# One attention order on one core: first unit turned by VectorE alone, scores by halves, fewer and longer weighing groups

## The chip, the cores and the metric

The kernel runs on one core of a Trainium2 chip. The metric is the device time of the whole program in microseconds (us), read over several runs. Within the core, TensorE (PE; its weight loads are listed apart as PEld) multiplies and transposes, VectorE (DVE), ScalarE (ACT) and GpSimd (POOL) do elementwise work, and SyncE (SP) issues every DMA, one after another, on one queue (SPq). Each engine works through its own list in order, so an instruction that waits holds up everything behind it on that engine.

## The reference, cut to what matters

Rotary attention over 4 batches and 8 heads of 576 positions and 64 dimensions, then two feed-forward stages on 2304 tokens:

```
q_rot, k_rot = rotate(q), rotate(k)                 # x1*cos - x2*sin, x1*sin + x2*cos
scores = q_rot @ k_rot^T / 8;  attn = softmax(scores)
x = (attn @ v) as 2304 x 512
h = x @ w_in; g = elu(h); x = g @ w_out             # 512 -> 2048 -> 512
out = ((x @ w1) * (x @ w2)) @ w3 @ w_out2           # 512 -> 1024 -> 512
```

All of it is float32. The kernel splits an operand into a rounded high part and a remainder (hi, lo) and multiplies hi*hi + hi*lo + lo*hi, which is why most products stand as three matmuls or as stacked operands.

## The kernel before, in words

The program has two stages. The attention stage (lines 140 to 509) has an order written out by hand; the feed-forward stage (from line 512) is placed by a planner and follows when the attention is nearly done. Only the attention stage is touched.

A **unit** is one batch and one pair of heads (j = 0, 1): there are 16, in the list `units`. A unit has nine **score groups** g = (unit, c, j): four blocks of 128 queries for each head, and one last group (c = 4) that takes the remaining 64 queries of both heads. The list `seq` has all 144 groups, and slot n of the loop at lines 496 to 509 belongs to `seq[n]`. In slot n the loop writes out, in this order: the copies of the last slot's transposes out of PSUM (`evacuate_all`, five of twelve on ScalarE, the rest on VectorE); the steps due first in slot n; in the first slots some warming matmuls on zeros (`FILL`, `warm_up`); the scores and softmax of group n + 2 (`AHEAD` = 2, and the score tiles `ps_s` have two buffers); the other steps due in slot n; the transposes of group n (`turn`, tile ptp, and ptl for the remaining 64 keys).

The softmax of a group is a maximum on VectorE (line 298, tile nm) and an exponential with its sum on ScalarE (line 302, tile pr). `norm` (lines 357 and 358) takes the reciprocal of the sums on VectorE, `spread` widens it on GpSimd (rb, line 84), `norm_turn` transposes that on TensorE (ptr), and `weigh` multiplies the turned probabilities with v into the tile o: line 392 for key blocks 0 to 3 (two heads beside each other, each 64 columns of the array), line 394 for the rest of both heads, line 397 for the 64 last queries. `weighed` scales o into xT on VectorE. `PV` says in which slot of a unit which key blocks are weighed, for the first half of the queries (256) and the second (320). Slots are counted from the unit's own first slot; slot 9 is slot 0 of the next unit.

The scores of units 1 to 15 read a stacked copy (`stack`, tile st) of the rotated q and k (hl): the hi and lo parts of one head are put above each other on 128 partitions by eight DMAs per unit from SBUF to SBUF (lines 260 and 263). Only unit 0, and the last group of each unit, read hl itself (line 278); unit 0 does so with 64 rows of the array.

The rotation is done by GpSimd for units 2 to 15 (`rope`, tile raw_qk: two multiplications, line 184, an addition, line 187; then ScalarE rounds to hi, line 80, and GpSimd subtracts for lo, line 193). `ROPE` gives the slots of these five steps for q and for k, relative to the unit before. Before, k's remainder is due in slot 2 and q's in slot 4, and the eight DMAs of the stack follow in slot 4 (`STACK`). Unit 0 is rotated by pieces (`first_rope`, `part`): k's columns 0 to 352 and q's 0 to 256 by VectorE, k's columns 420 to 640 and q's 256 to 576 by GpSimd, k's 352 to 420 by VectorE. Unit 1's k is rotated by GpSimd, its q by VectorE.

SP's queue also carries the loads of q and k two units ahead (`LOAD_QK`, line 167, ring of three buffers, so a load waits until an older tile has been read), v (line 171), and one block of feed-forward weights per unit (line 91), which ScalarE, VectorE and GpSimd convert in six steps (`paced`, `STEPS`).

At the very start TensorE runs 27 warming matmuls (two passes each) on a tile of zeros while the first loads and rotations run.

## Time and profile before

| | |
|---|---|
| device time, three runs | 1053.31 us median, 1046.85 to 1053.48 |
| profiled execution | 1052.59 us, span 1050.8 us |
| busy share: PE, PEld, DVE, ACT, POOL | 99%, 82%, 54%, 44%, 25% |
| chain that ended last | PE 90%, SPq 3%, DMA 3%, DVE 1%, POOL 1% |
| attention stage | from the start to 320 us of the span, its end among the first feed-forward work |

The span runs from the first to the last instruction of one profiled execution; 1.79 us of its own time lie around it. Shares are means over two unlike stages. In the attention stage four engines and the DMA queues work side by side, in the feed-forward stage TensorE works almost alone. "Idle before" names what an engine waited for; a wait is charged to what came last. Busy time of TensorE includes the filling and emptying of its pipeline, so the distance from one start to the next is the better measure of what a group of matmuls costs.

### The profile page before, as it was taken

How to read it: one execution, taken by the hardware profiler on the slowest of the kernel's cores; microseconds unless marked ns; L12 is line 12 of the kernel's file. 1: busy time of each engine (PE TensorE's matmuls, PEld its weight loads, DVE VectorE, ACT ScalarE, POOL GpSimd, SP SyncE). 2: the span in 40 equal slices, each digit the busy share in tenths (PEclk: the TensorE clock that was granted, in tenths of full speed). 3: DMA queues.
4: the chain of work that ended last, by engine and by line, in shares of the span. 5: the costliest groups of instructions: out<-in, count | busy, mean ns of one | idle time of the engine just before them, and what ended most of it. 6: DMA issues, size and time to landing. Idle time of an engine off the chain costs nothing.

```text
span 1050.8 us, 14641 instructions
## 1 busy us (share of the span) xinstructions
PE 1037.8 (99%) x5590; PEld 865.4 (82%) x5590; DVE 568.3 (54%) x978; ACT 463.7 (44%) x921; POOL 257.9 (25%) x260
## 2 busy tenths in 40 slices
PE   8999999999999999999999999999999999999998
PEld 7767767777777888888888999989888888889997
DVE  4678878778767996668667653212313214122321
ACT  2567666667546756556545644322211212112121
POOL 4698889888510010001000000000100000000000
PEclk7799999999999999999999999999999999999999
DMA  4687878786756015545555523536400101001000
GB/s 157 190 233 213 232 221 216 211 236 198 172 211 242 1 40 180 180 160 180 181 180 180 181 101 127 193 120 220 143 0 1 41 1 41 1 1 41 1 31 31
DMA packets 46390, 138.84 MB, mean 132 GB/s; under 512 B 5488, under 2 KB 7152, under 8 KB 46320
## 3 DMA queue, kind: packets, MB, share of 16 engines
q1 hardware_dynamic: 46320, 137.91, 41.6%
q8 instruction: 44, 0.72, 0.3%
q14 instruction: 26, 0.21, 0.1%
HBM read 85.66 MB, written 25.69 MB: 106 GB/s over the span
## 4 chain that ended last, share of the span: by engine, by line
PE 90%; SPq 3%; DMA 3%; DVE 1%; POOL 1%; issue 1%; ACTq 0%; ACT 0%; DVEq 0%
PE h L537 19%; PE y L564 19%; PE a L537 9%; PE b L537 9%; PE y L674 9%; PE ptp L334 6%; PE o L392 5%; PE s L286 5%; PE w L615 4%; DMA st<-hl 3%; PE s L278 2%; SPq L263 2%; SPq L260 1%; PE o L394 1%; POOL hl L193 1%
## 5 line engine op out<-in xcount | busy, mean ns | idle before, releaser
L537 PE MATMUL h<-xt,w 128*128 128x512 f32 (+1 forms) x960 | 213.4, 368 | 0.0
L564 PE MATMUL y<-g,w 128*128 128x512 f32 (+1 forms) x960 | 212.5, 367 | 0.0
L537 PEld LDWEIGHTS h<-xt,w 128*128 128x128 f32 x960 | 175.2, 188 | 23.4 <-DVE e L552 0.2
L564 PEld LDWEIGHTS y<-g,w 128*128 128x128 f32 x960 | 175.2, 188 | 22.5
L76 POOL TENSOR_TENSOR xt<-xT,xt 128x512 fp32r<-128x512 f32 (+1 forms) x20 | 26.5, 1326 | 668.9 <-DVE xt L82 668.1
L302 ACT ACTIVATE pr<-s,nm 128x576 f32<-128x576 f32 x144 | 107.0, 743 | 100.8 <-DVE nm L298 99.9
L661 DVE TENSOR_TENSOR a<-b,a 128x512 f32<-128x512 f32 (+1 forms) x40 | 25.5, 637 | 180.0 <-PE b L537 180.0
L298 DVE TENSOR_REDUCE nm<-s 128x1 f32<-128x576 f32 x144 | 108.6, 754 | 25.7 <-PE s L286 11.7
L537 PE MATMUL a<-xt,w 128*128 128x512 f32 (+1 forms) x480 | 107.4, 368 | 0.0
L537 PE MATMUL b<-xt,w 128*128 128x512 f32 (+1 forms) x480 | 106.8, 367 | 0.0
L674 PE MATMUL y<-W,g 128*128 128x512 f32 x432 | 104.9, 390 | 0.0
L334 PEld LDWEIGHTS ptp<-idt,pr 128*128 128x128 f32 x576 | 63.4, 144 | 46.2 <-issue 23.7
L286 PE MATMUL s<-st 128*128 128x288 f32 x480 | 94.9, 316 | 4.4 <-DMA st<-hl 4.3
L537 PEld LDWEIGHTS a<-xt,w 128*128 128x128 f32 x480 | 88.2, 188 | 12.5
L537 PEld LDWEIGHTS b<-xt,w 128*128 128x128 f32 x480 | 87.7, 188 | 11.3
L334 PE MATMUL ptp<-idt,pr 128*128 128x128 f32 x576 | 96.4, 291 | 0.0
L674 PEld LDWEIGHTS y<-W,g 128*128 128x128 f32 x432 | 80.9, 188 | 16.1
L659 ACT ACTIVATE a<-a 128x512 f32<-128x512 f32 (+1 forms) x40 | 22.3, 556 | 139.2 <-PE a L537 139.2
L552 DVE SCALAR_TENSOR_TENSOR e<-e,h 128x512 f32<-128x512 f32 (+1 forms) x80 | 50.3, 631 | 61.1 <-ACT e L550 60.7
L184 POOL TENSOR_TENSOR raw_qk<-raw_qk,tab 128x640 f32<-128x640 f32 (+1 forms) x56 | 82.5, 1483 | 2.3
L549 ACT ACTIVATE e<-h 128x512 f32<-128x512 f32 (+1 forms) x80 | 44.2, 554 | 72.6 <-PE h L537 70.2
L286 PEld LDWEIGHTS s<-st 128*128 128x128 f32 x480 | 67.9, 189 | 7.0 <-issue 3.8
(301 smaller groups left out, 1275.0 us busy)
## 6 DMA issues: line engine op xcount, KB each, us to landing
kept<-w SPq DMA_DIRECT2D x40, 512.0 KB, 2.6
w<-kept SPq DMA_DIRECT2D x40, 512.0 KB, 3.3
st<-hl SPq DMA_DIRECT2D x60, 288.0 KB, 4.5
raw<-w_ SPq DMA_DIRECT2D x32, 512.0 KB, 3.6
raw_qk<-k_ SPq DMA_DIRECT2D x15, 640.0 KB, 6.1
raw_qk<-q_ SPq DMA_DIRECT2D x15, 576.0 KB, 5.1
st<-hl SPq DMA_DIRECT2D x60, 144.0 KB, 4.2
raw<-w_in_ SPq DMA_DIRECT2D x16, 512.0 KB, 5.1
```

What stands on the lines that cost most here:

```text
L184: pool.tensor_tensor(r[:, z], r[:, z], tab[:, w, z, TAB[w]], op=ALU.mult)
L286: pe.matmul(s[:, n, :288], st[:, j, 0, c * P:c * P + P], st[:, j, z, n * 288:(n + 1) * 288], start=(z == 1), stop=(z == 2),)
L298: dve.tensor_reduce(nm, s[:, :, :288], axis=AX.XY, op=ALU.max, negate=True)
L302: act.activation(pr_t[u, c][:, j].rearrange("p (n i) -> p n i", n=2), s[:, :, :288], ACTF.Exp, bias=nm, accum_out=sums_t[u, hf][:, at_:at_ ...
L334: pe.transpose(pt[:, kc], pr[:, at_:at_ + P], idt)
L392: pe.matmul(o[64 * j:64 * j + 64], vj[:, j, kc], th[:, j, kc], start=(kc == 0), stop=False)
L537: pe.matmul(ps[:, :n], w[:, a, cc * P:(cc + 1) * P], x[cc][:, c], start=(i == 0), stop=(i == 11))
L549: act.activation(e, ps[:, :n], ACTF.Relu, scale=-1.0)
L552: dve.scalar_tensor_tensor(g, e, -1.0, ps[:, :n], op0=ALU.add, op1=ALU.max)
L564: pe.matmul(ys[ti][o][:, :n], wout[f][:, a, o * P:(o + 1) * P], g[:, c], start=(f == 0 and i == 0), stop=(f == NF - 1 and i == 2),)
L615: pe.matmul(ps, w3_t[i, j // 4][:, a, j % 4 * P:j % 4 * P + P], wo[j][:, c], start=(j == 0 and n == 0), stop=(j == 7 and n == 2),)
L674: pe.matmul(outs[ti][o], g[:, a, o * P:(o + 1) * P], wW[f][:, c], start=(f == 0 and i == 0), stop=(f == NG - 1 and i == 2),)
```

## The change

The order of the attention stage is rewritten in these places. Unit 0 is rotated by VectorE alone. `scores` runs the three products of one half of the keys before those of the other half, and in the very first group four warming matmuls stand between the halves; there are 30 instead of 27 warming matmuls at the start and 4, 2, 2, 2, 2 instead of 4, 2, 2 in the first slots. The stack is filled by twelve DMAs of 144 KB: eight for k right after k's remainder (now due two slots before the unit ahead begins), four for q right after q's remainder (slot 3). Each load of q or k follows the stack's DMAs that set its buffer free. The weighing goes from four groups per half to two, with the rest of the keys inside the second, in slots 6, 8, 10 and 12; the last 64 queries use 128 rows, half of them zeros. Tile o has one buffer, the transposes three. `norm` and the first `spread` come one slot later, and the weights' conversion is spread over slots 0 to 10 of its run.

```diff
@@ -25,26 +25,25 @@
 
 
 
-NORM = (2, 7)
-SPREAD = (3, 9)
+NORM = (3, 8)
+SPREAD = (4, 9)
 NTURN = (5, 11)
 PV = (
-    (5, 0, (0,)), (6, 0, (1,)), (7, 0, (2, 3)), (8, 0, (4,)),
-    (10, 1, (0,)), (11, 1, (1,)), (12, 1, (2, 3)), (13, 1, (4,)),
+    (6, 0, (0, 1)), (8, 0, (4, 2, 3)), (10, 1, (0, 1)), (12, 1, (4, 2, 3)),
 )
 LOAD_V = 6
-LOAD_QK = 4
-ROPE = ((-1, 0, 1, 1, 4), (-5, -4, -3, -3, 2))
-STACK = 4
+FIRST_LOADS = ((0, 2, 1), (3, 2, 0), (5, 3, 1))
+ROPE = ((-1, 0, 1, 1, 3), (-5, -4, -3, -3, -2))
+DIAG = 5
 
 FIRST = ((0, 1, 4), (0, 0, 0, 1, 2), (0, 0, 3, 3, 4), 2)
-KD = 420
-WARM = 27
-FILL = (4, 2, 2)
+WARM = 30
+FILL = (4, 2, 2, 2, 2)
+FILL_IN = 4
 EVAC_ACT = (1, 0, 0, 1, 0, 0, 0, 0, 1, 0, 1, 0)
 
 
-PF, PF_AT, PF_STEP, STEPS, DLEAD = 6, 10, 9, (0, 1, 2, 2, 3, 8), 6
+PF, PF_AT, PF_STEP, STEPS, DLEAD = 6, 10, 9, (0, 2, 5, 7, 8, 10), 6
 NA = 2 * PF
 
 EARLY, EARLY_STEP, STAGES = 17, 1, 3
@@ -150,12 +149,13 @@
         x_p = pool1("x", 2)
         sm_p = pool1("sm", 4)
         ps_s = c1.enter_context(tc.tile_pool(name="ps_s", bufs=2, space=PSUM, reuse_waits="tile"))
-        ps_o = c1.enter_context(tc.tile_pool(name="ps_o", bufs=2, space=PSUM, reuse_waits="tile"))
-        ps_t = c1.enter_context(tc.tile_pool(name="ps_t", bufs=2, space=PSUM, reuse_waits="tile"))
+        ps_o = c1.enter_context(tc.tile_pool(name="ps_o", bufs=1, space=PSUM, reuse_waits="tile"))
+        ps_t = c1.enter_context(tc.tile_pool(name="ps_t", bufs=3, space=PSUM, reuse_waits="tile"))
 
         tab = tab_p.tile([P, 2, 2, SK], F32, name="tab")
         diag = [cst.tile([P, 2, P], F32R, name=f"diag{i}") for i in range(2)]
         two = cst.tile([P, D], F32, name="two")
+        pl1 = cst.tile([P, 384], F32, name="plT1")
         zero = cst.tile([P, 1, 1], F32, name="zero")
         rb = [cst.tile([P, 2, 2, D], F32, name="rb"), cst.tile([P, 3, 2, D], F32, name="rb2")]
 
@@ -191,8 +191,11 @@
 
             def low():
                 pool.tensor_tensor(lo, r[:, 0], hi.bitcast(F32), op=ALU.subtract)
-                if w == 0:
-                    diagonal(u)
+                stack(u, w)
+
+                m = units.index(u) + 2 - w
+                if m < len(units):
+                    load(units[m], 1 - w)
 
             return [lambda: turn(0), lambda: turn(1), add, high, low]
 
@@ -235,9 +238,7 @@
         def first_rope(u):
             for w, at_, to, eng, steps in (
                 (1, 0, 352, dve, (0, 1, 2)), (0, 0, 256, dve, (0, 1, 2)),
-                (1, 0, 352, dve, (3, 4)), (0, 0, 256, dve, (3, 4)),
-                (1, KD, SK, pool, (0, 1, 2)), (1, 352, KD, dve, (0, 1, 2)), (1, 352, SK, dve, (3, 4)),
-                (0, 256, S, pool, (0, 1, 2)),
+                (1, 0, 352, dve, (3, 4)), (0, 0, 256, dve, (3, 4)), (1, 352, SK, dve, (0, 1, 2, 3, 4)),
             ):
                 pieces = part(u, w, at_, to, eng, act, eng)
                 for k_ in steps:
@@ -249,18 +250,17 @@
                 h = slice(64 * j, 64 * j + 64)
                 copy_hi(diag[units.index(u) % 2][h, :, h], hls[u][h, :, 512:S].bitcast(F32), pool)
 
-        def stack(u):
-
-            st = stacks[u] = st_p.tile([P, 2, 3, S], F32R, tag="st", name="st")
+        def stack(u, w):
+
+            if u not in stacks:
+                stacks[u] = st_p.tile([P, 2, 3, S], F32R, tag="st", name="st")
+            st = stacks[u]
             for j in range(2):
-                c = (SK, S)[j]
-                for e in range(2):
-                    part = hls[u][64 * j:64 * j + 64, e].bitcast(F32)
-                    both = part[:, :2 * c].rearrange("p (w c) -> p w c", w=2)[:, :, :S]
-                    nc.sync.dma_start(st[64 * e:64 * e + 64, j, 0:2].bitcast(F32), both)
-                for e in range(2):
-                    part = hls[u][64 * j:64 * j + 64, 1 - e].bitcast(F32)
-                    nc.sync.dma_start(st[64 * e:64 * e + 64, j, 2].bitcast(F32), part[:, c:c + S])
+                c = (0, (SK, S)[j])[w]
+                for z in ((0,), (1, 2))[w]:
+                    for e in range(2):
+                        part = hls[u][64 * j:64 * j + 64, (e, 1 - e)[z == 2]].bitcast(F32)
+                        nc.sync.dma_start(st[64 * e:64 * e + 64, j, z].bitcast(F32), part[:, c:c + S])
 
 
         HALF = ((0, 256), (256, 320))
@@ -273,8 +273,10 @@
 
                 d, h = diag[units.index(u) % 2], slice(64 * j, 64 * j + 64) if c < 4 else slice(0, P)
                 at_ = S + 64 * (c == 4 or j == 0)
-                for i, (a, e) in enumerate(PAIRS):
-                    for n in range(2):
+                for n in range(2):
+                    if n and g == seq[0]:
+                        warm_up(FILL_IN)
+                    for i, (a, e) in enumerate(PAIRS):
                         pe.matmul(
                             s[:, n, :288], hls[u][h, a, c * P:c * P + P] if c < 4 else d[:, a],
                             hls[u][h, e, at_ + n * 288:at_ + (n + 1) * 288], start=(i == 0), stop=(i == 2),
@@ -325,7 +327,7 @@
             if j == 0 and c in (0, 2):
                 pt_t[u, hf] = [
                     pt_p.tile([P, 2, 4, nq], F32, tag=f"pt{hf}", name="ptT"),
-                    pt_p.tile([P, nq + 64 * hf], F32, tag=f"pl{hf}", name="plT"),
+                    pl1 if hf else pt_p.tile([P, nq], F32, tag="pl0", name="plT"),
                 ]
             (th, tl), pr = pt_t[u, hf], pr_t[u, c].rearrange("p j i -> p (j i)")
             pt = ps_t.tile([P, 4, P], F32, tag="pt", name="ptp")
@@ -380,25 +382,28 @@
 
         o_t = {}
 
-        def weigh(n, u, hf, kc):
+        def weigh(n, u, hf, kcs):
             nq = HALF[hf][1]
-            if kc == 0:
+            if kcs[0] == 0:
                 o_t[u, hf] = ps_o.tile([P, nq], F32, tag="o", name="o", padded_shape=[P, 512])
             o = o_t[u, hf]
             th, tl = pt_t[u, hf]
             vj = vs[u][:, :2 * NKC * D].rearrange("p (j k d) -> p j k d", j=2, k=NKC)
-            if kc < 4:
+            for kc in kcs:
+                if kc == 4:
+                    pe.matmul(o[:, :256], vs[u][:, 2 * NKC * D:], tl[:, :256], start=False, stop=False)
+                    if hf:
+
+                        for j in range(2):
+                            pe.matmul(
+                                o[64 * j:64 * j + 64, 256:], vj[:, j, 4], tl[:, 256 + 64 * j:320 + 64 * j],
+                                start=False, stop=False,
+                            )
+                    continue
                 for j in range(2):
-                    pe.matmul(o[64 * j:64 * j + 64], vj[:, j, kc], th[:, j, kc], start=(kc == 0), stop=False)
-                return
-            pe.matmul(o[:, :256], vs[u][:, 2 * NKC * D:], tl[:, :256], start=False, stop=not hf)
-            if hf:
-                for j in range(2):
-                    pe.matmul(
-                        o[64 * j:64 * j + 64, 256:], vj[:64, j, 4], tl[:64, 256 + 64 * j:320 + 64 * j],
-                        start=False, stop=True,
-                    )
-            at(n + 1, weighed, u, hf)
+                    pe.matmul(o[64 * j:64 * j + 64], vj[:, j, kc], th[:, j, kc], start=(kc == 0), stop=(kc == 3))
+            if kcs[-1] == 3:
+                at(n + 1, weighed, u, hf, first=True)
 
         def weighed(u, hf):
             n0, nq = HALF[hf]
@@ -419,7 +424,7 @@
 
             at(max(0, n - DLEAD), fetch)
             for i, d in enumerate(STEPS):
-                at(n + d, step, i, first=i in (0, 4, 5))
+                at(n + d, step, i, first=i in (0, 4))
 
         units = [(b, hp) for b in range(B) for hp in range(4)]
         order = [(c, j) for c in range(4) for j in range(2)] + [(4, 0)]
@@ -431,36 +436,36 @@
 
         for i, u in enumerate(units):
             n = 9 * i
-            if i + 2 < len(units):
-                at(n + LOAD_QK, load, units[i + 2], 1)
-                at(n + LOAD_QK, load, units[i + 2], 0)
+            if i == 0:
+                for d, ahead, w in FIRST_LOADS:
+                    at(d, load, units[ahead], w)
             if i + 1 < len(units):
                 v_ = units[i + 1]
                 at(n + LOAD_V, load_v, v_)
                 if i == 0:
                     steps = part(u, 0, 256, S, dve, act, dve)
-                    for k_ in (3, 4):
-                        at(FIRST[0][k_ - 3], steps[k_])
+                    for k_ in range(5):
+                        at(FIRST[0][max(k_ - 3, 0)], steps[k_])
                     at(FIRST[0][2], diagonal, u)
                     for w in (1, 0):
                         steps = part(v_, w, 0, (S, SK)[w], (dve, pool)[w], act, (dve, pool)[w])
                         for k_, d in enumerate(FIRST[2 - w]):
                             at(d, steps[k_])
                     at(FIRST[2][4], diagonal, v_)
-                    at(FIRST[2][4], stack, v_)
+                    at(FIRST[1][4], stack, v_, 1)
+                    at(FIRST[2][4], stack, v_, 0)
                 else:
                     for w in (1, 0):
                         at(n + ROPE[w][0], lambda v_=v_, w=w: steps_of.__setitem__((v_, w), rope(v_, w)))
                         for k_, d in enumerate(ROPE[w]):
                             at(n + d, lambda v_=v_, w=w, k_=k_: steps_of[v_, w][k_]())
-                    at(n + STACK, stack, v_)
+                    at(n + DIAG, diagonal, v_)
             for hf in range(2):
                 at(n + NORM[hf], norm, u, hf)
                 at(n + SPREAD[hf], spread, u, hf)
                 at(n + NTURN[hf], norm_turn, u, hf)
             for t, hf, kcs in PV:
-                for kc in kcs:
-                    at(n + t, weigh, n + t, u, hf, kc)
+                at(n + t, weigh, n + t, u, hf, kcs)
         at(4, lambda: pool.tensor_tensor(two, idt[:, :D], idt[:, D:], op=ALU.add))
         at(FIRST[3], lambda: pool.tensor_scalar(tab[:, 0], tab[:, 1], SCALE, 1.0, op0=ALU.mult, op1=ALU.mult))
         for i in range(2 * PF):
@@ -489,6 +494,7 @@
                 copy_hi(d, zero.to_broadcast([P, 2, P]), pool)
             first_rope(units[0])
             pool.memset(rb[1][:, 2], 0.0)
+            pool.memset(pl1[64:, 256:], 0.0)
             for g in seq[:AHEAD]:
                 scores(g)
                 softmax(g)
```

## Rows read from the trace of the kernel before

**Rows 1.** Windows: length, busy us (instructions) per engine, PEclk, DMA share, GB/s.
```profile
10.00:20.00 10.00, 7.38 (x31) 6.46 (x32) 5.25 (x8) 2.36 (x6) 7.58 (x8) 0.60 0.27 91
20.00:30.00 10.00, 10.00 (x40) 8.33 (x38) 6.03 (x11) 3.92 (x10) 3.73 (x5) 0.50 0.39 123
30.00:40.00 10.00, 10.00 (x41) 7.06 (x40) 4.99 (x8) 3.62 (x10) 6.15 (x7) 0.54 0.66 148
...
150.00:200.00 50.00, 48.69 (x353) 35.41 (x351) 39.64 (x73) 34.00 (x79) 42.52 (x41) 1.00 0.78 214
...
11.00:12.00 1.00, 0.00 (x0) 0.00 (x0) 0.97 (x2) 0.00 (x0) 0.95 (x2) 0.97 0.00 0
```

**Rows 2.** Timeline of the first 45 us: start, length, engine, line, work.
```profile
1.05 8.22 PE L475 MATMUL warm<-warm 128*128 128x128 f32 x54 [1.05 <-DVE warm L486]
9.21 0.40 PE L278 MATMUL s<-hl 64*128 64x288 f32 x1
9.74 1.48 DVE L215 TENSOR_TENSOR raw_qk<-raw_qk,tab 128x68 f32<-128x68 f32 x2
12.62 2.46 PE L278 MATMUL s<-hl 64*128 64x288 f32 x11 [3.02 <-ACT hl L80]
...
19.53 1.42 DVE L215 TENSOR_TENSOR raw_qk<-raw_qk,tab 128x576 f32<-128x576 f32 x2
...
40.07 0.76 PE L286 MATMUL s<-st 128*128 128x288 f32 x4
```

**Rows 3.** Timeline of TensorE in the steady units.
```profile
63.05 0.76 PE L392 MATMUL o<-ptT,v__388 128*64 128x320 f32 x4
...
188.44 0.76 PE L392 MATMUL o<-ptT,v__2018 128*64 128x320 f32 x4
...
203.80 0.78 PE L286 MATMUL s<-st 128*128 128x288 f32 x4
204.41 0.66 PE L334 MATMUL ptp<-idt,pr 128*128 128x128 f32 x4
204.83 0.76 PE L286 MATMUL s<-st 128*128 128x288 f32 x4
205.52 0.76 PE L392 MATMUL o<-ptT,v__2251 128*64 128x320 f32 x4
206.21 0.66 PE L334 MATMUL ptp<-idt,pr 128*128 128x128 f32 x4
...
209.50 1.30 PE L392 MATMUL o<-ptT,v__2251 128*64 128x320 f32 x8
210.73 0.66 PE L334 MATMUL ptp<-idt,pr 128*128 128x128 f32 x4
...
211.97 0.59 PE L394 MATMUL o<-plT,v__2251 128*128 128x256 f32 x2
212.49 0.33 PE L397 MATMUL o<-plT,v__2251 64*64 64x64 f32 x4
...
292.67 0.76 PE L392 MATMUL o<-ptT,v__3405 128*64 128x320 f32 x4
```

**Rows 4.** Waits from 40 to 300 us: us in total, times, longest.
```profile
PE s L286 <- DMA st<-hl: 4.3, 10, 0.9
...
POOL rb L84 <- DVE ri L358: 35.2, 22, 8.0
```

**Rows 5.** DMA issues of the page: KB each, median us from issue to landing.
```profile
st<-hl SPq DMA_DIRECT2D x60, 144.0 KB, 4.2
```

**Rows 6.** Stack DMAs on SP's queue, 60 to 300 us: issue ns min/median/max.
```profile
L260 SPq DMA_DIRECT2D st<-hl x52: 596/638/984, 66.2 to 283.3; - x52
...
L263 SPq DMA_DIRECT2D st<-hl x52: 597/1242/1450, 68.7 to 285.3; - x52
```

**Rows 7.** Costliest groups of the page: busy us, mean ns, idle before.
```profile
L302 ACT ACTIVATE pr<-s,nm 128x576 f32<-128x576 f32 x144 | 107.0, 743 | 100.8 <-DVE nm L298 99.9
...
L298 DVE TENSOR_REDUCE nm<-s 128x1 f32<-128x576 f32 x144 | 108.6, 754 | 25.7 <-PE s L286 11.7
```

## The prediction

> **What bounds the kernel now.** I read the windows by stretch first, then the timeline of the start, then TensorE's timeline and the waits in the steady part. The windows show that the attention has two regimes. From about 11 us to nearly 40 us the granted clock is 0.50, the 1.2 GHz level, while TensorE is busy all the time from 12.62 us on; in the steady windows it is 1.00 [rows 1, 2]. The timeline shows how the clock was lost: the warming matmuls end at 9.27 us, one score matmul follows, and then TensorE waits 3.02 us for ScalarE's rounding of k's second part; the clock falls inside that gap. Unit 1's first scores come at 40.07 us, 27.45 us after the restart [rows 2].
>
> In the steady part TensorE sets the pace. The first group of a unit's second half comes at 63.05 us and 13 units later at 292.67 us, so a unit takes 17.66 us; one without a wait takes 17.08 us (188.44 to 205.52) [rows 3]. The difference, 0.58 us a unit or 7.6 us over the 13, is TensorE late for the stacked operands: the only wait listed for it is on st, 4.3 us in ten pieces, and the rest hides in the pipeline's ends [rows 4]. GpSimd is busy 42.52 of 50 us, VectorE 39.64, ScalarE 34.00, the DMA engines 0.78 [rows 1]: per unit of 17.66 us that is 15.0, 14.0, 12.0 and 13.8 us. Nothing else is at its limit, but GpSimd and VectorE are near enough to matter if TensorE gets faster. After the attention TensorE is always fed, so what the attention saves should arrive whole at the end.
>
> The sum below is made against the profiled execution, 1052.59 us, which is 0.72 us under the median of the runs shown. About 1% of it, 10.5 us, is what a measurement can tell from no change.
>
> **The start.** VectorE now turns all of unit 0. Before, its two multiplications of only 68 columns took 1.48 us while GpSimd worked on its own pieces, as long as two of 576 columns at 19.53 us (1.42 us) [rows 2]. Without GpSimd beside it I estimate a multiplication of 288 columns at 0.4 us (half of 0.71, and a little). Three such steps, the rounding and the remainder put k's second part at about 11 to 11.5 us. The first half's three matmuls run at about 9.9 us (three more warming matmuls, 6 passes of 0.09 to 0.15 us, end the warming there), four more warming matmuls fill to about 11.3 us, and the second half follows. So the 3.02 us gap nearly closes, the first two groups end near 13 us instead of 15.08, and the clock should stay at 1.00.
>
> How long does unit 0 then take? TensorE's 27.45 us of work at half clock would be about 14 us, and the fillers add about 1 us. But VectorE's list did not get shorter: from 10 to 40 us it worked 5.25 + 6.03 + 4.99 = 16.3 us [rows 1], it gains q's second part (four steps of 320 columns, some 1.8 us) and loses about 1 us of stretched pieces, so some 17 us. It begins its maxima at about 12 us, works in order, and has q's second part and two multiplications of unit 1's q (1.42 us) between the maxima of groups 2 and 3. TensorE will idle about 1.5 to 2 us there. I put unit 1's first scores at 30 us: 12 plus 17 of VectorE's work plus 1 of waiting. **That is minus 10 us**, with ends of 0 (the clock falls anyway where it fell) and minus 13 (TensorE's own 15 us).
>
> **The stack.** After q's remainder SP now issues four DMAs where it issued eight. Eight cost 4 x 0.64 + 4 x 1.24 = 7.5 us before the last was even issued, and a 144 KB one lands 4.2 us later [rows 5, 6]; four cost 2.6 to 5.0 us, and the first pair, which is all the first scores need of q, lands about 5.5 us after the remainder. The remainder also comes a slot sooner. From slot 3 to slot 7, where the scores need it, there are four slots or 7.5 us. The wait goes: **minus 7.6 us**, at worst nothing. All twelve issues are 7.7 us at the short price and 14.9 at the long one; four other loads at about 0.6 us make that 10 to 17.3 us a unit. I take the middle, since the long ones come where many are in flight at once and the change spreads them: SP is not the bound (at the long price it would be, by 0.3 us a unit or 4 us in all). The loads moved behind the stack wait for nothing any more, since their buffer was read just before.
>
> **The weighing.** A group of four matmuls with 64 columns takes 0.69 us from its start to the next start, a group of eight 1.23 us: two fours cost 0.15 us more than one eight. Scores followed by such a group take 0.69 us, followed by transposes 0.61: 0.08 us to get in [rows 3]. So every change into and out of that form costs 0.23 us, and the new order has one less in each half: 0.46 us. The last four small matmuls, 0.33 us in a form of their own, join the group and should cost about 0.2 us less with their entry; I take 0.15. Together 0.61 us a unit, over some 15 units **minus 9 us**; the ends are 0 and minus 13.
>
> **New waits.** The weighing now sits in slots 1, 3, 6 and 8 of the nine; a slot without it is scores and transposes, 0.61 + 0.42 = 1.03 us [rows 3]. A score tile is free again after scores (0.78), maximum (0.754) and exponential (0.743) [rows 3, 7], 2.28 us and with three hand-overs some 2.5 us, and must be within two slots. Slots 4 and 5 (the latter with 0.2 us of transposed sums) are 2.3 us, and VectorE has copies and the scaling into xT ahead of the maximum there. I get 0.3 to 0.7 us of new idle time per unit behind slot 5; the long slot 3 before may hide all of it. I take 0.5 us for 14 units: **plus 7 us**, ends 0 and plus 10. VectorE's own sum, 14.0 us a unit, is unchanged; its weight conversions now fall into the long slots 3, 6 and 8. Tile o with one buffer costs nothing: it is read at the head of slots 4 and 0, and written again two slots and one slot later. Three buffers for the transposes cost nothing. The halves in `scores` move no work in later units. The zeros in the last group's 128 rows are one small fill.
>
> Sum: 1052.6 - 10 - 7.6 - 9 + 7 = **1033 us**. A steady unit is then 17.66 - 0.58 - 0.61 + 0.5 = 17.0 us, still above GpSimd's 15.0.
>
> **The clock, row against rule.** At half clock TensorE stayed at 100% busy from 20 to 30 us and did not get the clock back [rows 1]. The Trainium skill (TensorE: Matmul & The Clock Gate, What's actually happening) says that activity releases the throttle. The trace disagrees here: 27 us of unbroken work with 64-row scores and transposes left it at 0.50. By the page a fall in the start would soon be over and leave the sum near 1035 us, as an estimate; by the rows it lasts to the end of unit 0, which is the first rival's 1039.
>
> **Rivals.** *The clock falls after all*, in VectorE's pile-up at 18 to 20 us. For it: the rows just named show that unit 0's kind of work does not raise the clock, so it may not hold it. Against: the fall before came with 3 us of nothing, and here warming matmuls stand in five slots. Then the start gains 2 us up to group 1 and about 4 us more of faster work until 20 us, and pays the extra fillers at half clock (8 passes of 0.2 us, 1.7 us): about 4 us net. 1052.6 - 4 - 9.6 = 1039 us (1034 to 1045). Chance 0.22.
>
> *The steady part gains nothing*, because TensorE waits for VectorE and ScalarE about as long as it saved (0.58 + 0.61 = 1.2 us a unit). This is also the case in which changes of form were not what they seem. For it: 2.5 us of chain against 2.3 us of slots. Then only the start stays: 1043 us, or 1049 if the clock falls too. Chance 0.21.
>
> *GpSimd becomes the bound, and it gets slower.* k's remainder now stands directly behind k's addition in its list, and between them ScalarE must round k, behind whatever it is doing: 0.73 us of rounding plus up to an exponential and a copy, 1.5 to 2.1 us of idle GpSimd. Added to 15.0 us of work and the present 2.5 us of waiting for the sums (35.2 us over 14 units [rows 4]) a unit would take 19.6 us: 14 x 1.9 = 27 us more, less the 10 of the start, 1070 us. It decides from 19.1 us a unit on. Against it: the waits for sums are slack and should shrink first. Chance 0.05.
>
> **Numbers.** The forecast has 0.52 (own range 1024 to 1041). Range over all: 1024 to 1047, which leaves out the slow rival, the far end of the third case and a gain beyond all ends. Faster by over 1% (below about 1042): nearly all of the forecast, four fifths of the first rival, a quarter of the second, 0.73. Within 1%: 0.22. Slower: 0.05.
>
> **What will show it.** Granted clock 1.00 from 12 to 40 us, and unit 1's first scores near 30 us; 18 to 22 us is the place to look for a fall. No wait of TensorE on st. Thirteen units at about 17.0 us each; scores delayed on ScalarE's exponential behind slot 5. GpSimd's idle time before k's remainder under 1 us. A clock at 0.50 after 20 us, or units at 17.7 us, would make the sum wrong; units over 19 us its sign.

## The result and the profile after

The changed kernel takes 1041.43 us (median of 6 runs, 1039.91 to 1044.03) beside 1053.39 us for the kernel before on the same chip: a ratio of 0.9899, 95% interval 0.9871 to 0.9927. The profiled execution, 1039.91 us, is the fastest of the six and the only one with a mean granted clock of 1.000; the others have 0.992 to 0.996. So the rows below show the kernel in the one execution that kept its clock. Its span is 1038.1 us, 12.7 us under the one before.

**The start.** First the windows of the changed kernel (length, busy us per engine, PEclk, DMA share, GB/s); they answer to [rows 1].

```profile
10.00:20.00 10.00, 8.92 (x63) 7.29 (x61) 6.38 (x11) 3.78 (x9) 4.60 (x3) 1.00 0.30 103
20.00:30.00 10.00, 8.04 (x56) 6.92 (x56) 8.09 (x15) 6.23 (x14) 6.31 (x8) 1.00 0.75 193
30.00:40.00 10.00, 7.37 (x55) 5.39 (x54) 4.91 (x11) 4.32 (x9) 8.21 (x10) 1.00 1.01 303
150.00:200.00 50.00, 48.59 (x365) 37.30 (x365) 44.95 (x75) 36.19 (x82) 44.34 (x45) 1.00 0.82 234
```

The clock is 1.00, the 2.4 GHz level, where it was 0.50 to 0.60. In the last row VectorE has 44.95 us where it had 39.64.

The timeline of the same start, answering to [rows 2] (start, length, engine, line, work, in brackets the idle time before and what ended it):

```profile
1.05 9.47 PE L480 MATMUL warm<-warm 128*128 128x128 f32 x60 [1.05 <-DVE warm L491]
10.45 0.66 PE L280 MATMUL s<-hl 64*128 64x288 f32 x3
12.12 1.07 PE L280 MATMUL s<-hl 64*128 64x288 f32 x9
18.23 1.42 DVE L218 TENSOR_TENSOR raw_qk<-raw_qk,tab 128x576 f32<-128x576 f32 x2
20.23 0.48 DVE L234 SCALAR_TENSOR_TENSOR hl<-raw_qk,hl 128x320 fp32r<-128x320 f32 x1
...
20.77 0.79 PE L280 MATMUL s<-hl 64*128 64x288 f32 x4 [1.37 <-DVE hl L234]
21.84 6.00 SPq L263 DMA_DIRECT2D st<-hl  x8
27.88 0.60 SPq L167 DMA_DIRECT2D raw_qk<-q_  x1
28.58 2.49 SPq L263 DMA_DIRECT2D st<-hl  x4
...
28.58 0.44 PE L377 MATMUL ptr<-idt,rb 128*128 128x128 f32 x2 [1.19 <-POOL rb L83]
34.43 0.77 PE L288 MATMUL s<-st 128*128 128x288 f32 x4 [2.59 <-DMA st<-hl]
```

The 3.02 us gap is filled. Unit 1's first scores come at 34.43 us instead of 40.07. Three long waits stand ahead of them, 1.37 + 1.19 + 2.59 = 5.15 us; the last is for unit 1's own stack, which SP issues as eight DMAs for k, a load, and four for q.

**The steady part.** TensorE's timeline, answering to [rows 3]: first groups of the second halves of units 1 and 14, and parts of one unit in between, with one row of VectorE.

```profile
57.28 1.30 PE L404 MATMUL o<-ptT,v__403 128*64 128x320 f32 x8
...
177.96 1.30 PE L404 MATMUL o<-ptT,v__2050 128*64 128x320 f32 x8
...
180.60 0.60 PE L336 MATMUL ptp<-idt,pr 128*128 128x128 f32 x4
181.24 0.80 PE L288 MATMUL s<-st 128*128 128x288 f32 x4
...
186.17 0.60 PE L336 MATMUL ptp<-idt,pr 128*128 128x128 f32 x4
187.12 1.06 PE L280 MATMUL s<-hl,diag 128*128 128x288 f32 x6 [0.36 <-ACT pr L304]
...
194.35 0.77 PE L288 MATMUL s<-st 128*128 128x288 f32 x4
194.65 0.41 DVE L411 TENSOR_TENSOR xT<-o,R 128x256 f32<-128x256 f32 x1
195.21 1.30 PE L404 MATMUL o<-ptT,v__2286 128*64 128x320 f32 x8
...
280.47 1.30 PE L404 MATMUL o<-ptT,v__3457 128*64 128x320 f32 x8
```

(280.47 - 57.28) / 13 = 17.17 us a unit, where it was 17.66. The unit shown takes 17.25 us (177.96 to 195.21), and three waits stand in it, read from start to start. From 186.17 to 187.12 pass 0.95 us; scores follow transposes after 0.36 us where nothing is late (177.84 to 178.20 in the run without the addition, below), so TensorE waits 0.6 us for ScalarE's exponential. From 180.60 to 181.24 pass 0.64 us, a wait of 0.28. From 194.35 to 195.21 pass 0.86 us instead of 0.69 [rows 3], a wait of 0.17: VectorE has only just read the one tile o. That leaves about 16.2 us of TensorE's own work. The list of waits from 40 to 300 us, answering to [rows 4], names only the first of the three and has no wait on st:

```profile
PE s L280 <- ACT pr L304: 5.5, 15, 0.6
```

The 12.7 us add up as 5.6 (start), 0.1 (rest of unit 1's pipeline), 6.4 (13 units of 0.49) and 0.5 (after unit 14).

### The profile page after: what moved, and what is told of

Same layout as the page of the kernel before. It is cut to its first block, busy times and chain, and to the rows that moved or that the text cites. A ratio compares the mean times of both kernels' runs of the same rounds, so it can differ in the third digit from the quotient of the medians.

```text
span 1038.1 us, 14799 instructions
## 1 busy us (share of the span) xinstructions
PE 1020.0 (98%) x5612; PEld 860.6 (83%) x5612; DVE 582.9 (56%) x981; ACT 465.8 (45%) x921; POOL 249.3 (24%) x255
## 4 chain that ended last, share of the span: by engine, by line
PE 87%; DVE 8%; ACT 2%; issue 1%; SPq 1%; DMA 0%; POOL 0%; ACTq 0%; DVEq 0%
PE h L543 19%; PE y L570 19%; PE a L543 10%; PE b L543 9%; PE y L680 9%; PE o L404 5%; PE w L621 4%; PE ptp L336 3%; PE s L288 3%; DVE nm L300 2%; PE s L280 2%; DVE wr L112 1%; ACT pr L304 1%; DVE plT L320 1%; PE warm L480 1%
## 5 line engine op out<-in xcount | busy, mean ns | idle before, releaser
L288 PE MATMUL s<-st 128*128 128x288 f32 x480 | 92.8, 315 | 3.0 <-DMA st<-hl 2.6
L336 PE MATMUL ptp<-idt,pr 128*128 128x128 f32 x576 | 90.0, 279 | 0.0
```

Source lines behind the costliest of these rows:

```text
L288: pe.matmul(s[:, n, :288], st[:, j, 0, c * P:c * P + P], st[:, j, z, n * 288:(n + 1) * 288], start=(z == 1), stop=(z == 2),)
L336: pe.transpose(pt[:, kc], pr[:, at_:at_ + P], idt)
```

## The experiments

Unless said otherwise the edit is made on the changed kernel. "Scores" is the start of unit 1's first scores, "unit" the mean of 13 units, both from the profiled run; "holds" means a granted clock of 1.00 up to those scores and in them. The runs were made on several chips, and each ratio is to the kernel before on the same chip, whose medians lie between 1049.61 and 1053.39 us. So rows are compared by their ratios and their profiled runs, not by their medians, and two rows whose intervals overlap are not told apart by time.

| kernel | scores | unit | median us | ratio to before, 95% |
|---|---|---|---|---|
| before | 40.07 | 17.66 | 1053.39 | 1 |
| changed | 34.43, holds | 17.17 | 1041.43 | 0.9899 (0.9871 to 0.9927) |
| start alone | 38.84 | 17.50 | 1051.76 | 1.0005 (0.9985 to 1.0024) |
| stack alone | 38.48 | 17.68 | 1051.73 | 1.0006 (0.9990 to 1.0023) |
| no added fill | 35.08 | 17.16 | 1041.11 | 0.9912 (0.9885 to 0.9939) |
| early order of the stack | 38.44 | 17.17 | 1042.86 | 0.9922 (0.9896 to 0.9949) |
| four groups, old buffers | 41.11 | 18.00 | 1057.99 | 1.0069 (1.0047 to 1.0092) |
| old buffers | 38.42 | 17.50 | 1048.59 | 0.9975 (0.9959 to 0.9991) |
| slot 5 | 38.81 | 17.42 | 1044.60 | 0.9950 (0.9931 to 0.9968) |
| slot 5, weight steps | 35.28 | 17.34 | 1043.70 | 0.9933 (0.9911 to 0.9954) |
| no add | 34.62 | 16.81 | 1035.78 | 0.9863 (0.9844 to 0.9883) |
| no add, slot 5 | 38.19 | 16.99 | 1039.49 | 0.9889 (0.9866 to 0.9913) |
| q1 later | 33.57 | 17.16 | 1039.66 | 0.9895 (0.9876 to 0.9914) |
| joined | 32.20, holds | 16.80 | 1033.31 | 0.9833 (0.9811 to 0.9855) |

**The added warming matmuls taken out.**

```diff
-WARM = 30
-FILL = (4, 2, 2, 2, 2)
-FILL_IN = 4
+WARM = 27
+FILL = (4, 2, 2)
+FILL_IN = 0
```

> The changed kernel without its added warming matmuls: 27 at the start, 4, 2, 2 in the first slots, none between the halves of the first group. Theory: the added ones keep the clock; without them TensorE idles between the halves and again at 18 to 21 us, the granted clock falls to 0.50 for part of the first 40 us, and the time is 3 to 6 us above the changed kernel's 1041.4. Rival: scores by halves and VectorE alone are enough; the clock stays at 1.00, unit 1's first scores come at 34 us as in the changed kernel, and the time is within 1 us of it.

The time is that of the changed kernel, not the 3 to 6 us more of the theory. In the profiled run the clock falls as the theory said; its windows:

```profile
20.00:30.00 10.00, 9.65 (x36) 7.81 (x36) 6.36 (x12) 4.94 (x11) 4.08 (x7) 0.53 0.79 201
30.00:40.00 10.00, 10.00 (x64) 7.82 (x63) 6.68 (x12) 5.32 (x12) 8.65 (x10) 0.79 1.01 293
```

TensorE is busy 9.65 and 10.00 of 10 us, up to about 34 us at the 1.2 GHz level, yet the scores come at 35.08, only 0.65 us later than in the changed kernel at full clock: without the fillers TensorE has less to do, and what the changed kernel wins by its clock it spends in the three waits. Where the clock falls with the fillers in and stays down, as in the early order and in no add, slot 5 below, the scores come at 38.44 and 38.19. A gain from the fillers on the whole can't be seen: the ratios lie within each other's intervals, and five of the six executions of the changed kernel lost some of the clock with the fillers in.

**Four groups again, with the buffers of before.**

```diff
-    (6, 0, (0, 1)), (8, 0, (4, 2, 3)), (10, 1, (0, 1)), (12, 1, (4, 2, 3)),
+    (5, 0, (0,)), (6, 0, (1,)), (7, 0, (4,)), (8, 0, (2, 3)),
+    (10, 1, (0,)), (11, 1, (1,)), (12, 1, (4,)), (13, 1, (2, 3)),
```
and `ps_o` with 2, `ps_t` with 2 buffers.

> The changed kernel with the weighing in four groups per half again (slots 5, 6, 7, 8 and 10 to 13), o with two buffers and the transposes with two. Theory: TensorE's own work grows by 0.76 us a unit, but its waits behind the slots without weighing (about 0.9 us a unit in the trace of the changed kernel) go away: a unit 17.1 to 17.3 us as before, time within 2 us of 1041.4. Rival: the grouping is worth what was forecast for it alone, 9 us, and the waits have another cause: a unit near 17.9 us, time near 1050.

Units of 18.00 us, 0.83 more than in the changed kernel, and slower than the kernel before: the theory failed, and the rival is near with its unit, not with its time. The waits of TensorE from 60 to 280 us:

```profile
PE ptp L336 <- DVE plT L320: 10.7, 12, 0.9
```

The transposes wait 0.9 us a unit for VectorE's copies. So this is not the price of the forms alone.

**Old buffers alone.**

```diff
-ps_o bufs=1, ps_t bufs=3
+ps_o bufs=2, ps_t bufs=2
```

> The changed kernel with o in two buffers and the transposes in two, as before the change; the grouping of the weighing stays. Theory: the third transpose buffer carries much of the result. With two, the transposes at the turn of a unit wait for VectorE's late copies of ptl (its sums step and a weight step stand ahead of them), as the run with four groups showed: 0.5 to 0.9 us a unit, 1048 to 1054 us. Rival: the buffers were costed right at nothing; then one o buffer less costs only the 0.17 us a unit seen before the second half's first group, and this run gains 2 us: 1039.

Units of 17.50 us, 0.33 more than with three buffers, 4.3 us over 13. TensorE's waits from 60 to 280 us:

```profile
PE ptp L336 <- DVE plT L320: 4.2, 12, 0.4
PE ptp L336 <- DVE ptT L320: 3.6, 12, 0.3
```

Both are absent from the changed kernel. Of the 0.83 us of the run before, 0.33 thus comes with the buffers and 0.50 with the grouping, the waits of each included. The rest of the difference in time lies in the start: in this profiled run the clock fell in unit 0 and the scores come at 38.42.

**The first weighing in slot 5, alone and with the weight steps moved.**

```diff
-    (6, 0, (0, 1)), (8, 0, (4, 2, 3)), ...
+    (5, 0, (0, 1)), (8, 0, (4, 2, 3)), ...
 second run only:
-STEPS = (0, 2, 5, 7, 8, 10)
+STEPS = (0, 2, 4, 5, 8, 10)
```

> The changed kernel with the first weighing group of the first half in slot 5 instead of slot 6. Theory: TensorE waits before a unit's last score group (0.5 us) because slots 4 and 5 are shorter than scores, maximum and exponential in a row; with the group in slot 5 that wait goes, a unit falls from 17.2 to about 16.8 us and the time by 4 to 6 us to about 1036. Rival: VectorE and ScalarE set the pace of the unit, the wait moves to the next short slots, and the time stays within 1.5 us of 1041.4.

> The first weighing group in slot 5 as in the run that lost 3 us, and the weights' conversion steps of VectorE moved from slots 6 and 8 to slots 5 and 6 (STEPS 0, 2, 4, 5, 8, 10). Theory: that run lost because with one o buffer the second half's first group waited 0.7 us a unit for the scaling of the first half, which stood on VectorE behind the sums and the weight step of slot 8. With the weight step out of the way that wait falls to 0.1 us, the exponential's wait stays away, a unit takes 16.8 to 17.0 us and the time is 1036 to 1039. Rival: VectorE is simply full there (its sums step takes over 1 us beside GpSimd), the wait stays above 0.4 us, and the time is 1041 or more.

The first is slower than the changed kernel; the second has longer units (17.34 us), but its interval overlaps the changed kernel's. A row of TensorE's timeline in the first, and of its waits (60 to 280 us) in the second:

```profile
184.96 1.30 PE L404 MATMUL o<-ptT,v__2055 128*64 128x320 f32 x8 [0.65 <-ACT w L120]
```

```profile
PE s L288 <- ACT pr L304: 11.6, 13, 1.1
```

Alone, the exponential's wait nearly goes, but the weighing then waits until VectorE has multiplied the one tile o into xT (the row names ScalarE, which had long been done). With the weight steps moved the weighing no longer waits, but the wait is on the exponential again, 0.9 us a unit. Both theories failed. The slot only chooses which queue behind VectorE TensorE meets.

**Unit 1's k and its stack earlier (early order of the stack).**

```diff
-FIRST_LOADS = ((0, 2, 1), (3, 2, 0), (5, 3, 1))
-FIRST = ((0, 1, 4), (0, 0, 0, 1, 2), ...
+FIRST_LOADS = ((2, 2, 1), (5, 2, 0), (6, 3, 1))
+FIRST = ((0, 1, 4), (0, 0, 0, 0, 1), ...
```

This moves the rounding and the remainder of unit 1's k one slot ahead and the loads behind the stack, so that k's stack goes out sooner.

> The changed kernel with unit 1's k rounded in slot 0 and its remainder in slot 1 (so its eight stack DMAs start earlier), and the loads of unit 2's k and q and unit 3's k moved behind the stack's DMAs (slots 2, 5, 6). Theory: unit 1's first scores wait 2.6 us for the stack because SP's queue issues k's eight DMAs only from 21.8 us and a load before q's four; here they come 1 to 2.5 us earlier (32 to 33.4 us instead of 34.4) and the time falls by as much. Rival: the DMA engines are full at that time and what is moved ahead displaces the rest, so unit 1's scores come no earlier and later units wait for their q and k: no gain, or a loss of 1 to 2 us.

GpSimd's remainder of k now runs while VectorE makes unit 0's q: that step takes 1.17 us instead of 0.48, TensorE's gap there 2.06 us instead of 1.37, and the clock falls to 0.50. At that clock TensorE comes to the stacked scores only at 38.44 us and finds no wait; k's DMAs are issued from 19.70 us, but q's end at 33.94 us, where they ended at 31.07. So the theory failed, and what the earlier stack alone is worth at full clock stays open.

**The start alone, and the stack alone, on the kernel before.**

```diff
 start:
-(1, KD, SK, pool, (0, 1, 2)), (1, 352, KD, dve, (0, 1, 2)), ...
+(1, 352, SK, dve, (0, 1, 2, 3, 4)),
 with the halves in scores, WARM, FILL and FILL_IN of the change
 stack:
-    at(n + STACK, stack, v_)
+    stack(u, w), then the next load, behind each remainder
 with FIRST_LOADS, ROPE and DIAG of the change
```

> The kernel before with the change's start alone: unit 0 turned by VectorE, scores by halves, the added warming matmuls. The stack, its loads, the weighing and the weight steps stay as before. Theory: the sooner scores help little by themselves, because unit 1's first scores then wait for the stack's eight DMAs behind q's remainder; first scores of unit 1 near 37 to 38 us instead of 40.07, time 2 to 3 us below before. Rival: the start is worth its 5.6 us (34.4 us) whatever the stack does.

> The kernel before with the stack's part of the change alone: twelve DMAs, k's right after k's remainder two slots before the unit, the loads behind them, the later steps of q. Start, weighing, buffers and weight steps stay as before. Theory: TensorE's wait for the stacked operands in the steady part goes (7.6 us over 13 units, a unit 17.1 us) and the start does not change: 6 to 8 us below before. Rival: GpSimd, which now waits for ScalarE's rounding of k right behind the addition, falls behind and takes back half of it or more: 0 to 4 us below before.

Neither moves the time. With the start alone the clock fell in the profiled run (0.56 and 0.58 in the windows from 20 to 40 us) and the scores come at 38.84 with no wait for the stack ahead of them, so the reason that its theory gave was not tested. That execution, 1049.46 us, is one of the quicker of its ten. With the stack alone the wait on st is gone and the unit stays at 17.68 us, 0.6 more than the 17.08 of a unit without a wait. The time is the rival's, the way to it is not. Its timeline shows what took its place:

```profile
181.66 1.55 POOL L193 TENSOR_TENSOR hl<-raw_qk,hl 128x640 fp32r<-128x640 f32 x1 [0.85 <-ACT hl L80]
181.73 1.51 DVE L359 TENSOR_SCALAR ri<-sums 128x5 f32<-128x5 f32 x1
...
183.38 0.38 DVE L320 COPY plT<-ptl__2335 128x256 f32<-128x256 f32 x1
183.81 0.42 PEld L336 LDWEIGHTS ptp<-idt,pr 128*128 128x128 f32 x4 [0.51 <-DVE plT L320]
```

An addition to five columns of sums, 0.16 us where GpSimd is idle (at 37.44 us in the changed kernel), begins 0.07 us after GpSimd's remainder and ends with it, 1.51 us later. Behind it stands the copy that frees a transpose buffer, and TensorE waits for that copy. The Trainium skill (SBUF — State Buffer, SBUF: two separate sides) says that VectorE, in some of its operations, and GpSimd take a shared pair of ports for a whole instruction and the loser blocks; the trace agrees in these two rows. The edit itself brought the two beside each other. These are the groups of additions (busy us, mean ns), first of the kernel before from 45 to 292 us, then of the stack alone from 60 to 280 us:

```profile
L357 DVE TENSOR_SCALAR ri<-sums 128x5 f32<-128x5 f32 x14 | 8.4, 597 | 0.0
L357 DVE TENSOR_SCALAR ri<-sums 128x4 f32<-128x4 f32 x14 | 2.3, 162 | 0.2 <-ACT pr L302 0.2
```

```profile
L359 DVE TENSOR_SCALAR ri<-sums 128x5 f32<-128x5 f32 x12 | 18.0, 1503 | 0.0
L359 DVE TENSOR_SCALAR ri<-sums 128x4 f32<-128x4 f32 x13 | 12.2, 937 | 0.0
```

VectorE's order is that of the kernel before; only GpSimd's steps, the DMAs and the loads moved.

**The addition to the sums left out.**

```diff
-dve.tensor_scalar(ri, sums, 1e-9, None, op0=ALU.add)
-dve.reciprocal(ri, ri)
+dve.reciprocal(ri, sums)
```

> The changed kernel without the addition of 1e-9 to the sums of the exponentials (that addition is left out; the reciprocal is taken straight from the sums). Theory: VectorE's step on 5 columns of sums, which takes about 1 us in the mean beside GpSimd where alone it takes 0.16, stands ahead of the copies and maxima that TensorE waits for; without it two such stretches a unit go, the steady unit falls from 17.17 to 16.8 to 17.0 us and the time to 1036 to 1039 us. Rival: the stretch is a wait for GpSimd's running instruction that the next VectorE instruction inherits, or TensorE's 0.9 us of waits a unit are set by ScalarE's exponentials: the unit stays within 0.05 us of 17.17 and the time at 1040 to 1042 us.

As the theory had it: 16.81 us a unit, 1035.78 us. By time alone its interval still touches the changed kernel's, so the gain rests on the units: 0.36 us each, 4.6 us over 13. The groups of VectorE from 60 to 280 us (busy us, mean ns), first of the changed kernel, then of this one:

```profile
L359 DVE TENSOR_SCALAR ri<-sums 128x5 f32<-128x5 f32 x13 | 12.4, 950 | 0.0
L359 DVE TENSOR_SCALAR ri<-sums 128x4 f32<-128x4 f32 x13 | 11.0, 845 | 0.0
L115 DVE SCALAR_TENSOR_TENSOR wr<-raw,wr 128x512 int32<-128x512 int32 x11 | 7.2, 652 | 0.0
```

```profile
L115 DVE SCALAR_TENSOR_TENSOR wr<-raw,wr 128x512 int32<-128x512 int32 x11 | 17.7, 1614 | 0.0
L359 DVE RECIPROCAL ri<-sums 128x5 f32<-128x5 f32 x13 | 2.3, 177 | 0.0
```

The reciprocal, which reads the sums now, is not stretched: 177 ns. Part of the stretch moves on to the weight steps (L115 from 652 to 1614 ns), as the rival had it; but TensorE's list of waits names none of them. TensorE's timeline:

```profile
23.80 1.11 PE L336 MATMUL ptp<-idt,pr 128*128 128x128 f32 x4
...
27.20 0.66 PE L336 MATMUL ptp<-idt,pr 128*128 128x128 f32 x4
...
177.84 0.60 PE L336 MATMUL ptp<-idt,pr 128*128 128x128 f32 x4
178.20 0.78 PE L288 MATMUL s<-st 128*128 128x288 f32 x4
...
184.07 1.06 PE L280 MATMUL s<-hl,diag 128*128 128x288 f32 x6 [0.36 <-ACT pr L304]
...
191.29 0.77 PE L288 MATMUL s<-st 128*128 128x288 f32 x4
191.99 1.30 PE L403 MATMUL o<-ptT,v__2269 128*64 128x320 f32 x8
```

Two of the three waits of the changed kernel's unit are gone: 0.36 us where it had 0.64, and 0.70 from the scores to the weighing where it had 0.86. The third, for the exponential, is as long as before (0.36 idle in both lists of rows). The first two rows show the clock of unit 0: it fell at about 23 us, 2 us after the gap of 1.37 us and with TensorE busy, was back at 26 us (the same transposes take 1.11 us at 0.50 and 0.66 at 1.00), and was down once more from 30 to 33 us. The mean of the windows is 0.82 from 20 to 30 us and 0.84 from 30 to 40.

**The same with slot 5.**

```diff
-    (6, 0, (0, 1)), (8, 0, (4, 2, 3)), ...
+    (5, 0, (0, 1)), (8, 0, (4, 2, 3)), ...
```

> As the run before (the same addition is left out), with the first weighing of a unit in slot 5 instead of slot 6. With the addition, slot 5 gave units of 17.59 us, because the weighing waited 0.7 us for xT, which VectorE wrote behind the sums step. Theory: without the step xT comes about 1 us sooner, the weighing's wait goes, slots 4 and 5 are no longer two short ones in a row, the exponential's wait shrinks too: units of about 16.8 us, 1035 to 1037 us. Rival: xT is late for another reason (the copies of the transposed sums or GpSimd ahead of it): units of 17.3 us or more, 1041 us or more.

Between the two: the unit falls from 17.42 to 16.99 us against the run with the addition, single units to 16.58, but slot 6 without the addition has the shorter units. In the profiled run the clock falls in the same gap in which it held for the changed kernel:

```profile
21.14 1.32 PE L280 MATMUL s<-hl 64*128 64x288 f32 x4 [1.37 <-DVE hl L234]
```

**Unit 1's q multiplications one slot later.**

```diff
-FIRST = ((0, 1, 4), (0, 0, 0, 1, 2), (0, 0, 3, 3, 4), 2)
+FIRST = ((0, 1, 4), (0, 0, 0, 1, 2), (1, 1, 3, 3, 4), 2)
```

> The changed kernel with unit 1's two q multiplications on VectorE moved from slot 0 to slot 1 of unit 0, behind q's remainder and the maxima that TensorE waits for. Theory: TensorE's gap at about 19 to 21 us, 1.4 us in the run whose clock held, shrinks to under 0.7 us, the clock stays at 1.00 in the profiled run, unit 1's first scores come at 34 us or sooner, and the time is 1038 to 1040 us. Rival: the same work piles up one slot later, the gap moves to 21 to 24 us with 1.4 us or more, the granted clock falls to 0.50 there, unit 1's first scores come at about 38 us, 1041 to 1044 us.

The 1.37 us gap is gone (0.51 us for ScalarE is left), the clock holds through it and the scores come at 33.57. But the wait for the stack stays, and there the clock falls now, as the length of the scores shows (1.30 us where the changed kernel's took 0.77):

```profile
33.57 1.30 PE L288 MATMUL s<-st 128*128 128x288 f32 x4 [2.78 <-DMA st<-hl]
```

The second half of unit 1 begins at 57.60 us, no sooner than 57.28, and the ratio is the changed kernel's (0.9895 beside 0.9899). The gap is as short as the theory said, but the clock did not hold and nothing was gained.

**Joined.** No addition, q1 later, and two edits on the last wait of the start: one load moved behind q's stack, six warming matmuls in the gap.

```diff
-FIRST_LOADS = ((0, 2, 1), (3, 2, 0), (5, 3, 1))
+FIRST_LOADS = ((0, 2, 1), (5, 3, 1))
-FILL = (4, 2, 2, 2, 2)
+FILL = (4, 2, 2, 2, 2, 0, 0, 6)
+                    at(FIRST[2][4], load, units[2], 0)   # behind q's stack
```

> Four edits on the changed kernel: the addition of 1e-9 to the sums left out (the reciprocal is taken straight from them), unit 1's q multiplications in slot 1, the load of unit 2's q behind q's four stack DMAs instead of ahead of them, and six more warming matmuls at the end of unit 0, where TensorE waits for the stacked operands. Theory: the steady unit stays at the 16.81 us of the run without the addition; with q's multiplications later the 1.4 us gap at 19 to 21 us is gone, the stack comes 0.6 us sooner (unit 1's first scores at about 33 us, where 34.6 was measured) and the warming keeps the granted clock at 1.00 through that last wait; 1033 to 1035 us. Rival: the clock falls in one of the gaps that are left (26 us, the transposed sums waiting for GpSimd), or the extra warming matmuls delay the scores: unit 1's first scores at 34.5 to 37 us and 1035.5 to 1038 us, no better than without the addition alone.

1033.31 us (1031.96 to 1034.16), faster than both kernels: its interval, 0.9811 to 0.9855, lies under the changed kernel's. TensorE's timeline and one window:

```profile
27.83 0.44 PE L376 MATMUL ptr<-idt,rb 128*128 128x128 f32 x2 [1.17 <-POOL rb L83]
...
30.95 1.50 PE L480 MATMUL warm<-warm 128*128 128x128 f32 x12
32.20 0.76 PE L288 MATMUL s<-st 128*128 128x288 f32 x4
...
55.20 1.30 PE L403 MATMUL o<-ptT,v__402 128*64 128x320 f32 x8
```

```profile
30.00:40.00 10.00, 10.00 (x80) 7.85 (x77) 5.33 (x11) 6.48 (x14) 8.83 (x9) 1.00 0.99 310
```

No idle time is left ahead of the stacked scores, where the six warming matmuls (twelve passes) now stand, and the clock is 1.00 throughout. Against the run without the addition, which lost its clock in unit 0, the second half of unit 1 begins 2.2 us sooner (55.20 and 57.36); by time alone the two intervals overlap. The two added edits were not run apart.

## Why the prediction came out as it did

Direction and range held: 1041.4 us lies in 1024 to 1047. The forecast itself, 1033 us, was 8 us too low. Of these, 1.5 us lie between the profiled execution and the median of the six; the other 7 are terms of the sum, which erred in both directions. That the steady unit came out at 17.17 us, near the forecast 17.0, is in part luck: TensorE's own work fell by more than forecast, and its waits grew by more.

- **The start, minus 10 us, was mis-sized**: minus 5.6 in the profiled run. Its step "12 plus 17 of VectorE's work plus 1 of waiting" ended with VectorE, but unit 1's first scores need the stack, which was costed for the steady units only: 6.0 us of issues for k, a load, then q's four, and TensorE waits 2.59 us. The transposed sums add 1.19 us that it did not count. The joined kernel, without the wait for the stack and with VectorE's pile-up moved, has its scores at 32.20.
- **The first rival is true in part.** It named VectorE's pile-up at 18 to 20 us as the place where the clock falls. The gap there is 1.37 us, just under the 1.5 to 2 us foreseen, and at this length the clock goes either way: it held in the changed kernel's profiled run and fell at that gap in no add, slot 5, and in no added fill, where another 0.99 us of waiting stands just ahead of it. The five other runs of the changed kernel have a mean clock under 1; that it fell at the same place in them is likely, not shown. Once lost, the clock did not always stay at 0.50 to the end of unit 0, as the prediction had it: in the early order and in no add, slot 5 it was back only after 37 us, in no add within 4 us. The Trainium skill (TensorE: Matmul & The Clock Gate, What's actually happening) says that activity releases the throttle. The rows of no add agree with it; the windows of no added fill speak against it, where 9.65 and 10.00 of 10 us busy brought the clock back only at about 34 us. What tells the two apart stays open.
- **The stack, minus 7.6 us, was right about the wait and wrong about the time.** The wait is gone in every kernel that has the edit, and alone the edit is worth nothing (ratio 1.0006): it brought GpSimd's steps beside VectorE's additions to the sums, 0.60 and 0.16 us in the mean before and 1.50 and 0.94 us after, and the copy behind them came late by as much as the stack had. The prediction did not ask what the moved steps of GpSimd do to VectorE.
- **The weighing, minus 9 us, was too small.** TensorE's own work fell from 17.08 us a unit to about 16.2 (17.25 less waits of 0.60, 0.28 and 0.17; 16.80 less 0.60 without the addition), 0.88 us instead of 0.61, or 13 us over 15 units, its far end. How much of it belongs to the grouping and how much to the third transpose buffer is not shown.
- **New waits, plus 7 us, were too small**: 17.17 - 16.2, about 1.0 us a unit instead of 0.5, some 14 us over 14. The place that was foreseen, the exponential behind the two slots without weighing, has 0.6 us. The step that failed is "VectorE's own sum is unchanged": it is 44.95 / 50 x 17.17 = 15.4 us a unit instead of 14.0, and the additions to the sums went from 0.60 and 0.16 us in the mean to 0.95 and 0.85. What stands behind them, the maxima and the scaling into xT, comes late, and two more waits arise, 0.28 and 0.17 us in the unit shown. Without the addition both are gone and the unit is 0.36 us shorter.
- **The buffers, costed at nothing, were not nothing.** Taking both back costs 0.33 us a unit, although the single tile o alone costs about 0.17 (194.35 to 195.21); by the difference the third transpose buffer carries about 0.5 us, an estimate. That buffer, the later `norm` and `spread` and the spread weight steps were not run alone.
- **The slow rival** did not come. Its handshake is there: GpSimd is idle 0.85 us ahead of k's remainder in the row of the stack alone. The changed kernel has room for it, with GpSimd at 44.34 of 50 us busy.

## What to carry to other kernels

A wait that is named in a list is worth its length only if nothing else is late just behind it, and if the edit makes nothing late itself; ask of the engine next in line, with its instructions at the length they will have beside their new neighbours, before the gain is added. Parts of a reordering that are worth nothing alone (start, stack) can be worth 1% together with the buffers and grouping that let them through. After closing a gap on a clock that is lost by waiting, close the next ones too: here moving one of them only moved the fall of the clock to the next.

## What the hardware showed that was not expected

- VectorE's addition to 5 columns took 1.51 us beside a GpSimd instruction, its reciprocal of the same columns 0.18 us in the mean: here it is the operation that decides, not how much it reads.
- The same 1.37 us of waiting, after the same matmuls, left the granted clock at 1.00 in the changed kernel's profiled run and took it to 0.50 in no add, slot 5.
- The five executions of the changed kernel that lost part of the clock (means of 0.992 to 0.996) took 0.6 to 4.1 us longer than the one that kept it: 1040.55 to 1044.03 us beside 1039.91.
